# The scaled attention output is split by token, and a DMA transposes its halves

## The chip, the core and the metric

The kernel runs on one core of one Trainium2 chip. The metric is device time in microseconds (us) of one execution. Engines are named as in the profile: PE is TensorE, DVE is VectorE, ACT is ScalarE, POOL is GpSimd, and SP is the queue from which this kernel issues all its DMAs.

## The reference

Top-k attention over 4 batches, 8 heads, 576 tokens and a head width of 64, followed by two two-layer networks over the 2304 tokens (width 512, hidden width 2048):

```python
scores = scale * np.matmul(q, k.transpose(0, 1, 3, 2))
kth = np.partition(scores, -top_k, axis=-1)[..., -top_k:-top_k + 1]   # top_k = 32
scores = np.where(scores >= kth, scores, -1000000000.0)
attn = softmax(scores)                     # written out in the reference, with 1e-09 in the sum
x = (attn @ v) as (2304, 512)
x = np.maximum(x @ w_in1, 0.0) ** 2 @ w_out1
h = x @ w_in2
out = (h * np.clip(h + 3.0, 0.0, 6.0) / 6.0) @ w_out2
```

q, k and v are float32; the four weight matrices arrive as float64.

## The kernel before

**Precision.** Each matmul operand is scaled by a power of two and split into two fp16 halves, high and low; a product is the sum of three fp16 matmuls (high by high, high by low, low by high).

**Attention.** The tokens of a batch are cut into four blocks of 128 and one of 64. A block has 8 tiles (one head, 128 rows), a 64-token block 4 (two heads stacked): 144 tiles in all. A tile goes through PE (`qk`, L769), ACT (`evac`, L775), DVE (`topk`: four MAX8 and three MATCH_REPLACE8, L783 to L791, then `lowest`, L800), ACT (`below`, L805), POOL (`mask`, L808), ACT (`expo`, L813; `high`, L819), POOL (`low`, L823 and L824), a DMA transpose on SP (`wflip`, L828, into a buffer `wT`), and PE (`av`, L842).

**The operand of the first network.** `x_operand` turns a block's attention output into the operand `hl`, with features on the partitions. There are 20 blocks. Before the change: ACT copies the output head by head out of PSUM (L912), PE transposes it into a PSUM bank `misc` (`xflip`, L921), ACT squares it (L927), PE adds the squares over the features with four matmuls by a matrix of ones into a bank `h` (`xtotal`, L932), DVE takes the largest sum over the tokens (L936) and makes a power of two of it (L263 to L265), ACT scales the transposed values (L965) and makes the high half (L968), and POOL makes the low half (L971).

**The networks.** Two 64-token blocks share one unit, so there are 18 units of 128 tokens. For each unit `up` (L1091) makes four hidden blocks in one of the two PSUM banks `h`, ACT and DVE apply the function (L1098 to L1113), POOL makes the low half (L1116), and `acc` adds the second product (L1126 in the first network, L1134 in the second). Between the two networks `x2_operand` does for the unit what `x_operand` does for a block, without a transpose; its sum of squares is one matmul with one column (L1016).

**Weights.** At the start DVE turns the float64 words into float32 (L364 to L367) with help from ACT (L410) and POOL (L414), PE sums squares for a scale (L430), and PE, ACT and POOL split the matrices into halves.

**What sets the order.** `Plan` holds every step as a task with an engine, a cost and buffers to take, and runs through them with a priority from the table `PRIO` (an offset and a slope in the tile's or unit's number): whenever an engine is free, the ready task of lowest priority value whose buffers are free goes next. What comes out is a fixed order of instructions on each engine, SP included. On the chip each engine keeps that order, and an instruction that waits holds up everything behind it on its engine.

```python
    pool("wT", WTB, [P, 2 * S // P, P], F16)
    pool("x", XBUFS, [P, H, D], F32)
    for name, n in (("av", 1), ("misc", 1), ("h", 2)):
        pool(name, n, [P, 512], F32, ps)
```

Of the kernel before, what the change touches and what calls it, by code (L numbers as in the profile page):

```python
# [10 lines left out]
F16 = mybir.dt.float16  # L11
# [8 lines left out]
P = 128  # L20
# [12 lines left out]
class Plan:  # L33
# [101 lines left out]
def tile_topk_attention_moe_moe2(  # L135
# [36 lines left out]
    ones16 = const.tile([P, P], BF16, name="ones16")  # L172
    nc.gpsimd.memset(ones16, 1.0)
# [57 lines left out]
    pool("ghl", GBUFS, [P, 2, 512], F16)  # L231
    pool("m", 4, [P, TOPK], F32, st)
# [13 lines left out]
    def act(n):  # L246
        return 0.08 + 0.00086 * n
# [636 lines left out]
    def x_operand(i):  # L884
# [21 lines left out]
        def copy():  # L906
            box["x"] = x = take("x")
            a_ = T["av", i]
            for t in range(ntl):
                for hh in range(2 if tail else 1):  # L910
                    rows = slice(hh * TAIL, hh * TAIL + TAIL) if tail else slice(0, P)
                    nc.scalar.activation(x[0:n, 2 * t + hh if tail else t, :], a_[rows, t * D:(t + 1) * D], AF.Copy,  # L912
                                         scale=box["rv"][rows, t:t + 1])

        def flip():
            if o == 0:
                T["hl", u] = take("hl")
            box["pt"] = take("misc", "pt").rearrange("p (c n) -> p c n", c=KD)[:, :, 0:n]
            x = box["x"].rearrange("p h d -> p (h d)")
# [3 lines left out]
        def part(a):  # L923
            return T["hl", u][:, a, :, o:o + n]

        def square():
            nc.scalar.activation(part(1).bitcast(BF16), box["pt"], AF.Square)  # L927

        def total():
            box["pn"] = take("h", "pnx")[:, 0:n]  # L930
            for c in range(KD):
                nc.tensor.matmul(box["pn"], ones16, part(1).bitcast(BF16)[:, c, :], start=c == 0, stop=c == KD - 1)  # L932

        def scale():
            y = take("xy")
            nc.vector.tensor_reduce(y, box["pn"], axis=AX.X, op=ALU.max)  # L936
            T["sx", i], T["px", i] = take("scx"), take("px")
            scale_pair(y, T["px", i], EXP_P, T["sx", i])
# [6 lines left out]
        t3 = task("ACT", 1.6, ("xcopy", first[i]), copy, deps=[t2, *avs], alloc=["x"])  # L945
        free("rv", t1, t3)
        free("av", avs[0], t3)
        t4 = task("PE", 0.44 if not tail else 0.3, ("xflip", first[i]), flip, deps=[t3, hl_task.get(u)],
                  alloc=["misc"] + (["hl"] if o == 0 else []))
        hl_task.setdefault(u, t4)  # L950
        free("x", t3, t4)
        t5 = task("ACT", act(4 * n), ("xsquare", first[i]), square, deps=[t4])
        t6 = task("PE", mm(KD, n), ("xtotal", first[i]), total, deps=[t5], alloc=["h"])
        t7 = task("DVE", 0.65, ("xscale", first[i]), scale, deps=[t6], alloc=["xy", "scx", "px"])
        free("h", t6, t7)
        free("xy", t7, t7)
        scale_task[i] = t7
        if (SX if i else SX0) == "d":
            l_, = split(4 * n, lambda: box["pt"], [lambda: part(0)], [lambda: part(1)], lambda: T["sx", i], "d",
                        (("xhigh", first[i]), ("xlow", first[i])), [t7])  # L960
            free("misc", t4, l_)
        else:
            def evac():
                box["y"] = take("f", "y").rearrange("p (c n) -> p c n", c=KD)[:, :, 0:n]
                nc.scalar.activation(box["y"], box["pt"], AF.Copy, scale=T["sx", i])  # L965

            def high():
                nc.scalar.activation(part(0), box["y"], AF.Copy)  # L968

            def low():  # L970
                nc.gpsimd.tensor_tensor(part(1), box["y"], part(0), op=ALU.subtract)  # L971

            t8 = task("ACT", act(4 * n) + 0.09, ("xevac", first[i]), evac, deps=[t7], alloc=["f"])
            free("misc", t4, t8)
            t9 = task("ACT", act(4 * n), ("xhigh", first[i]), high, deps=[t8])
            l_ = task("POOL", gps(4 * n), ("xlow", first[i]), low, deps=[t9])
            free("f", t8, l_)
# [294 lines left out]
def first_of(order, b):  # L1272
# [16 lines left out]
SX = 'a'  # L1289
SX0 = 'a'  # L1290
# [3 lines left out]
WTB = 3  # L1294
# [9 lines left out]
    "load0": (79.38, 0.002),  # L1304
    "load1": (505.67, 1.218),
    "load2": (-131.52, 0.003),
    "load3": (-742.35, 0.015),
    "conv0": (-318.82, 2.010),
    "bits0": (15.78, 1.944),
    "add0": (40.24, 0.042),  # L1310
    "gram0": (150.09, 4.901),
    "conv1": (-402.12, 2.168),
    "bits1": (62.78, 1.548),
    "add1": (-314.29, 16.236),
    "gram1": (-177.84, 0.701),
    "conv2": (-322.11, 0.202),
    "bits2": (169.55, 0.060),
    "add2": (28.40, 0.397),
    "gram2": (37.78, 3.746),
    "conv3": (-319.50, 17.808),  # L1320
    "bits3": (-1197.31, 17.209),
    "add3": (-924.51, 132.166),
    "gram3": (-337.51, 0.363),
    "norm": (162.88, 3.211),
    "high0": (17.00, 4.877),
    "low0": (-407.54, 0.099),
    "scaled0": (1601.72, 0.274),
    "rest0": (124.60, 2.815),
    "high1": (39.66, 0.582),
    "low1": (363.86, 5.940),  # L1330
    "scaled1": (-638.88, 0.490),
    "rest1": (309.81, 6.499),
    "high2": (-353.82, 10.969),
    "low2": (525.93, 0.745),
    "scaled2": (1277.25, 0.112),
    "rest2": (497.91, 0.025),
    "high3": (328.67, 0.002),
    "low3": (323.86, 20.953),
    "scaled3": (12.56, 0.347),
    "rest3": (-296.43, 0.212),  # L1340
    "qsquare": (394.64, 3.096),
    "qtotal": (-522.30, 1.796),
    "qscale": (125.99, 6.115),
    "ksquare": (-651.27, 0.007),
    "ktotal": (-269.97, 0.040),
    "kscale": (60.65, 12.061),
    "vsquare": (-636.46, 0.206),
    "vtotal": (75.79, 0.095),
    "vscale": (1408.81, 257.879),
    "clear": (-435.69, 0.309),  # L1350
    "kload": (-205.24, 0.102),
    "vload": (360.66, 0.741),
    "qload": (-298.49, 5.036),
    "qhigh": (-487.53, 4.251),
    "qlow": (466.63, 0.760),
    "khigh": (-716.41, 2.774),
    "klow": (-745.17, 5.318),
    "vhigh": (-259.52, 0.835),
    "vlow": (371.44, 0.013),
    "kflip": (-237.83, 0.002),  # L1360
    "qscales": (357.31, 5.406),
    "qflip": (-3100.27, 1.015),
    "qk": (-92.22, 0.128),
    "evac": (-217.65, 0.005),
    "topk": (463.92, 4.188),
    "bias": (532.21, 0.398),
    "lowest": (-289.40, 0.274),
    "below": (6.46, 3.277),
    "mask": (-252.11, 1.195),
    "expo": (862.15, 0.942),  # L1370
    "whigh": (717.42, 0.312),
    "wlow": (749.09, 0.067),
    "wflip": (-709.67, 0.008),
    "av": (164.55, 0.248),
    "xinv": (692.76, 0.068),
    "xscales": (209.04, 12.568),
    "xcopy": (-199.03, 0.051),
    "xflip": (-261.41, 0.066),
    "xsquare": (-883.08, 0.591),
    "xtotal": (-1192.44, 0.731),  # L1380
    "xscale": (13.67, 0.378),
    "xevac": (-571.14, 1.046),
    "xhigh": (30.26, 0.684),
    "xlow": (-392.23, 0.138),
    "common": (166.36, 0.361),
    "ysquare": (37.42, 7.183),
    "ytotal": (-968.65, 0.540),
    "yscale": (-150.95, 4.882),
    "yhigh": (61.82, 2.649),
    "ylow": (-23.74, 0.008),  # L1390
    "whole": (37.32, 0.817),
    "up0": (568.05, 3.995),
    "up1": (500.02, 46.668),
    "relu0": (-966.40, 1.173),
    "relu1": (-180.07, 2.665),
# [39 lines left out]
```

## Time and profile before

| | |
|---|---|
| median of 3 runs | 1182.12 us (1181.19 to 1182.57) |
| the profiled execution | 1180.5 us |
| its span, first to last instruction | 1178.7 us |
| PE, DVE, ACT, POOL busy | 89%, 84%, 79%, 71% of the span |
| HBM read, written | 48.23 MB, 4.72 MB |

A busy share is the union of an engine's instructions. Matmuls overlap one another (each lasts some 0.2 us while a new one starts every 0.06 us), so the pace of PE is read from the distance between starts. The wait of an instruction is given behind it as the idle time of its engine and what ended it.

### The profile page before, as it was taken

How to read it: one execution, taken by the hardware profiler on the slowest of the kernel's cores; microseconds unless marked ns; L12 is line 12 of the kernel's file. 1: busy time of each engine (PE TensorE's matmuls, PEld its weight loads, DVE VectorE, ACT ScalarE, POOL GpSimd, SP SyncE). 2: the span in 40 equal slices, each digit the busy share in tenths (PEclk: the TensorE clock that was granted, in tenths of full speed). 3: DMA queues.
4: the chain of work that ended last, by engine and by line, in shares of the span. 5: the costliest groups of instructions: out<-in, count | busy, mean ns of one | idle time of the engine just before them, and what ended most of it. 6: DMA issues, size and time to landing. Idle time of an engine off the chain costs nothing.

```text
span 1178.7 us, 36919 instructions
## 1 busy us (share of the span) xinstructions
PE 1051.4 (89%) x14792; PEld 862.5 (73%) x14792; DVE 988.8 (84%) x2319; ACT 925.6 (79%) x1868; POOL 835.3 (71%) x1113
## 2 busy tenths in 40 slices
PE   2375688878999999999999999999989999999998
PEld 1232336776788788889787978888777978888885
DVE  4989899998995999999989999999978999998101
ACT  6589599899798878788888878888887787877432
POOL 5858868699775677777867787786766778777321
PEclk9997699988999999999999999999999999999999
DMA  9888754423554343445464443445463334333100
GB/s 235 234 249 244 225 156 119 104 48 65 90 97 102 79 75 55 75 74 98 78 118 84 71 74 56 72 62 92 86 110 55 66 65 80 62 60 61 12 11 19
DMA packets 276764, 112.50 MB, mean 95 GB/s; under 512 B 257520, under 2 KB 265712, under 8 KB 276592
## 3 DMA queue, kind: packets, MB, share of 16 engines
q1 hardware_dynamic: 276592, 110.14, 45.2%
q8 instruction: 116, 1.90, 0.7%
q14 instruction: 56, 0.46, 0.1%
HBM read 48.23 MB, written 4.72 MB: 45 GB/s over the span
## 4 chain that ended last, share of the span: by engine, by line
PE 53%; ACT 18%; DVE 9%; POOL 8%; issue 6%; DMA 5%; SPq 1%; ACTq 0%; DVEq 0%; POOLq 0%
PE hb L1091 21%; PE acc L1134 12%; PE acc L1126 11%; PE sp L769 4%; PE av L842 3%; POOL E L808 2%; ACT E L813 2%; DVE W L788 2%; ACT x L912 2%; POOL wc L823 2%; ACT S L775 2%; DVE m L791 1%; DVE cv L364 1%; DMA kT<-kn 1%; ACT w L541 1%
## 5 line engine op out<-in xcount | busy, mean ns | idle before, releaser
L1091 PE MATMUL hb<-hl,w 128*128 128x128 f16 x6912 | 456.2, 219 | 4.8 <-ACT stg L410 1.4
L1091 PEld LDWEIGHTS <-w 128*128 128x128 f16 x6912 | 411.4, 98 | 50.7 <-issue 6.4
L791 DVE MAX8 m<-W 128x8 f32<-128x576 f32 x432 | 326.0, 755 | 8.3
L1126 PE MATMUL acc<-ghl,w 128*128 128x128 f16 x3456 | 243.5, 221 | 5.3 <-ACT ghl L1113 2.6
L1134 PE MATMUL acc<-w,ghl 128*128 128x512 f16 x864 | 231.5, 379 | 11.7 <-DVE hl L279 7.5
L808 POOL TENSOR_TENSOR E<-S,E 128x576 f32<-128x576 f32 x144 | 204.3, 1419 | 48.5 <-ACT E L805 42.1
L1116 POOL TENSOR_TENSOR ghl<-r,ghl 128x512 f16<-128x512 f32 x144 | 169.4, 1177 | 93.5 <-ACT ghl L1113 85.3
L1126 PEld LDWEIGHTS <-w 128*128 128x128 f16 x3456 | 209.7, 99 | 17.6 <-issue 7.0
L788 DVE MATCH_REPLACE8 W<-m,W 128x576 f32<-128x576 f32 x288 | 213.8, 742 | 0.0
L823 POOL TENSOR_TENSOR wc<-E,wc 128x512 f16<-128x512 f32 x144 | 168.0, 1166 | 39.6 <-ACT wc L819 39.0
L775 ACT ACTIVATE S<-sp 128x576 f32<-128x576 f32 x144 | 93.5, 649 | 48.1 <-POOL E L808 40.0
L813 ACT ACTIVATE E<-E,scalars,scl 128x576 f32<-128x576 f32 x144 | 125.1, 869 | 4.4 <-POOL E L808 4.3
L805 ACT ACTIVATE E<-S,scalars 128x576 f32<-128x576 f32 x144 | 111.8, 776 | 19.0 <-DVE scalars L800 14.9
L783 DVE MAX8 m<-S 128x8 f32<-128x576 f32 x144 | 107.9, 750 | 18.9 <-ACT S L775 18.3
L769 PE MATMUL sp<-kT,qT 128*128 128x288 f16 (+1 forms) x640 | 100.1, 298 | 24.8 <-ACT S L775 20.0
L1134 PEld LDWEIGHTS <-ghl 128*128 128x128 f16 x864 | 74.9, 99 | 56.0 <-issue 16.0
L788 DVE MATCH_REPLACE8 W<-m,S 128x576 f32<-128x576 f32 x144 | 107.0, 743 | 0.0
L1106 DVE SCALAR_TENSOR_TENSOR r<-r,hb 128x512 f32<-128x512 f32 x72 | 49.0, 680 | 67.6 <-ACT r L1100 66.7
L1113 ACT ACTIVATE ghl<-r 128x512 f16<-128x512 f32 x144 | 90.5, 629 | 17.4 <-DVE r L1106 12.6
L819 ACT ACTIVATE wc<-E 128x576 f16<-128x576 f32 x144 | 98.5, 684 | 1.3
L795 POOL TENSOR_SCALAR scalars<-m,scl 128x1 f32<-128x1 f32 x144 | 38.5, 269 | 81.5 <-ACT E L813 32.2
L769 PEld LDWEIGHTS <-qT 128*128 128x128 f16 (+1 forms) x640 | 54.9, 103 | 51.8 <-issue 34.4
(130 smaller groups left out, 1493.5 us busy)
## 6 DMA issues: line engine op xcount, KB each, us to landing
w<-in_moe_w_in_dram SPq DMA_DIRECT2D x32, 512.0 KB, 4.9
w<-in_moe_w_out_dram SPq DMA_DIRECT2D x29, 512.0 KB, 4.4
out_dram<-o SPq DMA_DIRECT2D x16, 256.0 KB, 2.1
qf<-in_q_dram SPq DMA_DIRECT2D x31, 128.0 KB, 2.7
stg<-in_k_dram SPq DMA_DIRECT2D x12, 256.0 KB, 2.9
stg<-in_v_dram SPq DMA_DIRECT2D x12, 256.0 KB, 3.2
wT<-wc SPq DMA_TRANSPOSE x144, 3.2
stg<-in_moe_w_out_dram SPq DMA_DIRECT2D x6, 256.0 KB, 3.3
```

Source lines behind the costliest of these rows:

```text
L769: nc.tensor.matmul(dst, qT[:, 2 * ((2 * hp + hh) % 4) + a, 0:M], kflat[:, hh * SPAD + c * HALF:hh * SPAD + (c + 1) * HALF], start=a == 0, ...
L775: nc.scalar.activation(T["S", s].rearrange("p (c n) -> p c n", c=2), T["sp", s][:, :, 0:HALF], AF.Copy)
L788: nc.vector.match_replace(out=T["W", s], in_to_replace=m[:, 8 * c - 8:8 * c], in_values=T["S", s] if c == 1 else T["W", s], imm_value=-3.0e38)
L791: nc.vector.max(m[:, 4 * r:4 * r + 8], T["W", s])
L805: nc.scalar.activation(T["E", s], T["S", s], AF.Relu, bias=T["kb", s], scale=-FAR)
L808: nc.gpsimd.tensor_tensor(T["E", s], T["S", s], T["E", s], op=ALU.subtract)
L813: nc.scalar.activation(T["E", s], T["E", s], AF.Exp, bias=T["nb", s], scale=T["scl", ("q", i, half)][:, hp % 2:hp % 2 + 1], accum_out=T["s ...
L823: nc.gpsimd.tensor_tensor(wc[:, S + TAIL:], e[:, 0:S - TAIL], wc[:, 0:S - TAIL], op=ALU.subtract)
L1091: nc.tensor.matmul(box["h"][:, fi * n:(fi + 1) * n], wt[2 * m][:, kk * 4 + f // 4, a, f % 4 * P:(f % 4 + 1) * P], hl[:, c, kk, 0:n], start ...
L1116: nc.gpsimd.tensor_tensor(flat(box["g"][:, 1]), flat(box["r"]), flat(box["g"][:, 0]), op=ALU.subtract)
L1126: nc.tensor.matmul(flat_[:, c * w_:c * w_ + n], wt[1][:, f, a, c * P:(c + 1) * P], gl[d], start=(f, a, d) == (0, 0, 0) and c * w_ % 512 == ...
L1134: nc.tensor.matmul(o_, gl[d][:, ch * P:ch * P + rows], wt[3][:, f, a, :], start=f == 0 and (a, d) == (0, 0), stop=f == KF - 1 and (a, d) = ...
```

## The change

The operand keeps its tokens on the partitions until the end. ACT copies the output out of PSUM as before, squares all of it into a scratch tile and adds each token's squares on the way (`square`); PE adds the 128 tokens' sums with one matmul of one column (`total`), so that the norm is the sum of squares over the whole block instead of the largest token's; DVE makes the power of two (`scale`); ACT scales the copy in place (`scaled`) and makes the high half (`high`), POOL the low half (`low`), both into a new tile `xh`; and a DMA transpose on SP writes both halves, eight blocks of 128 by 128, into `hl` (`flip`). The transposes on PE and the DVE maximum are gone. `x` is held until `low` is done, the banks `misc` and `h` are taken for the one-column sum alone (`misc`) or not at all (`h`), and the buffers `wT` go from three to two. The path with `SX` is removed. All entries of `PRIO` are replaced.

```diff
+    pool("xh", XHBUFS, [P, 2, 512], F16)
...
+        def square():
+            box["xh"] = take("xh")
+            box["ss"] = take("ss")
+            nc.scalar.activation(box["xh"][0:n, 0].bitcast(BF16), rows(), AF.Square, accum_out=box["ss"][0:n])
+
+        def total():
+            box["pn"] = take("misc", "pnx")[:, 0:1]
+            nc.tensor.matmul(box["pn"], ones32[0:n, :], box["ss"][0:n], start=True, stop=True)
...
+        def scaled():
+            nc.scalar.activation(rows(), rows(), AF.Copy, scale=T["sx", i][0:n])
+
+        def high():
+            nc.scalar.activation(box["xh"][0:n, 0], rows(), AF.Copy)
+
+        def low():
+            nc.gpsimd.tensor_tensor(box["xh"][0:n, 1], rows(), box["xh"][0:n, 0], op=ALU.subtract)
+
         def flip():
...
-            for c in range(KD):
-                nc.tensor.transpose(box["pt"][:, c, :], x[0:n, c * P:(c + 1) * P], ident[0:n, 0:n])
...
+            nc.sync.dma_start_transpose(out=T["hl", u].rearrange("p a c n -> p (a c) n")[:, :, o:o + n],
+                                        in_=box["xh"][0:n].rearrange("p a n -> p (a n)"))
...
-        t6 = task("PE", mm(KD, n), ("xtotal", first[i]), total, deps=[t5], alloc=["h"])
+        t6 = task("PE", 0.2, ("xtotal", first[i]), total, deps=[t5], alloc=["misc"])
...
+        l_ = task("SP", 1.25, ("xflip", first[i]), flip, deps=[t10], lat=WLAT)
...
-WTB = 3
+WTB = 2
+XHBUFS = 1
...
-    "xflip": (-261.41, 0.066),
+    "xflip": (-58.53, 3.060),
```

**On PE**, where the last operand was transposed, before the change (`hb` and `acc` are the products of the second network of the units ahead; `w2`, `w3` its weights):

```order
L1091 LDWEIGHTS w2_88
L1091 MATMUL hb_20675<-hl_18739,w2_88 128x128
L921 MATMUL pt_20762<-ident_70,x_20718 128x128 x4
L1134 LDWEIGHTS ghl_20716
L1134 MATMUL acc_92<-w3_89,ghl_20716 128x512
```

And after the change, where the last operand's sum stands (L926 is the new `total`, L1080 and L1123 are the old L1091 and L1134):

```order
L1080 LDWEIGHTS w2_86
L1080 MATMUL hb_20537<-hl_18502,w2_86 128x128
L926 MATMUL pnx_20577<-scalars_83,ones32_75 128x1
L1123 LDWEIGHTS ghl_20471
L1123 MATMUL acc_90<-w3_87,ghl_20471 128x512
```

The four transposes, and the four matmuls by ones that followed some rows later, have become one matmul of one column.

**On SP**, near the end of the program, before the change (`wT` is a tile's transposed softmax weights, `o` the output of a unit):

```order
L828 DMA_TRANSPOSE wT_19735<-wc_19647 128x9x128
L828 DMA_TRANSPOSE wT_19849<-wc_19761 128x9x128
L828 DMA_TRANSPOSE wT_19994<-wc_19937 128x9x128
L1214 DMA out_0_dram<-o_20051 128x512
L828 DMA_TRANSPOSE wT_20102<-wc_20068 128x9x128
```

And after the change, with the operand of the block before the last (L942 is the new `flip`, L827 the old L828):

```order
L827 DMA_TRANSPOSE wT_19667<-wc_19617 128x9x128
L942 DMA_TRANSPOSE hl_19588<-xh_19623 128x8x128
L827 DMA_TRANSPOSE wT_19791<-wc_19727 128x9x128
L1203 DMA out_0_dram<-o_19854 128x512
L827 DMA_TRANSPOSE wT_19897<-wc_19831 128x9x128
```

The operand's transpose stands between two tiles' transposes, which wait behind it.

**On DVE**, around the scale of the first operand, before the change (`m` and `W` are of `topk`, `cv` of the weights' conversion, `w3` holds words of the last matrix):

```order
L791 MAX m_1430<-W_1531 128x8
L800 TENSOR_SCALAR scalars_85<-m_1430 128x1
L364 TENSOR_SCALAR cv_1620<-w3_89 128x512
L788 MATCH_REPLACE W_1623<-m_1508,S_1444 128x576
L367 SCALAR_TENSOR_TENSOR w3_89<-w3_89,cv_1620 128x512
L936 TENSOR_REDUCE scalars_85<-pnx_1626 128x1
L263 TENSOR_SCALAR scalars_85<-scalars_85 128x1
```

And after the change (L262 reads the one-column sum; L782 to L790 are `topk`):

```order
L790 MAX m_884<-W_968 128x8
L782 MAX m_1172<-S_992 128x8
L799 TENSOR_SCALAR scalars_83<-m_884 128x1
L787 MATCH_REPLACE W_1180<-m_963,S_946 128x576
L262 TENSOR_SCALAR scalars_83<-pnx_1183 128x1
L363 TENSOR_SCALAR cv_1199<-w3_87 128x512
L366 SCALAR_TENSOR_TENSOR w2_86<-w3_87,cv_1199 128x512
```

The scale stands earlier in the sequence of tiles, in front of conversions of the third matrix instead of the fourth, and the TENSOR_REDUCE ahead of it is gone.

## Rows read from the trace of the kernel before

**Rows 1.** The page, parts 1 and 2: busy shares, then tenths in 40 slices.

```profile
PE 1051.4 (89%) x14792; PEld 862.5 (73%) x14792; DVE 988.8 (84%) x2319; ACT 925.6 (79%) x1868; POOL 835.3 (71%) x1113
...
PE   2375688878999999999999999999989999999998
...
DVE  4989899998995999999989999999978999998101
```

**Rows 2.** Windows: length, then busy us (instructions) by engine, granted clock, DMA.

```profile
core 0: us, PE busy (x) PEld busy (x) DVE busy (x) ACT busy (x) POOL busy (x), PEclk, DMA share, GB/s
0.00:300.00 300.00, 200.56 (x1986) 137.71 (x1988) 262.15 (x599) 245.40 (x486) 232.29 (x288) 0.92 0.63 166
300.00:1090.00 790.00, 767.67 (x11708) 658.16 (x11708) 715.74 (x1693) 649.77 (x1327) 581.27 (x802) 1.00 0.44 78
1090.00:1178.70 88.70, 83.13 (x1105) 66.67 (x1102) 10.94 (x28) 30.46 (x56) 21.74 (x25) 0.99 0.07 14
```

**Rows 3.** Timeline of PE, 505 to 522: start, length, instruction, count.

```profile
508.75 0.83 PE L1126 MATMUL acc<-ghl,w 128*128 128x128 f16 x12
509.42 0.83 PE L1091 MATMUL hb<-hl,w 128*128 128x128 f16 x12
510.09 0.61 PE L921 MATMUL pt<-ident,x 128*128 128x128 f32 x4
510.54 0.65 PE L769 MATMUL sp<-kT,qT 128*128 128x288 f16 x4
...
511.70 0.39 PE L932 MATMUL pnx<-hl,ones 128*128 128x128 bf16 x4
511.92 0.83 PE L1126 MATMUL acc<-ghl,w 128*128 128x128 f16 x12
...
514.82 0.28 PE L1016 MATMUL pnx<-scalars,ones 128*128 128x1 f32 x2
514.96 1.46 PE L1134 MATMUL acc<-w,ghl 128*128 128x512 f16 x6
```

**Rows 4.** Windows for L921 alone: length, then busy us (instructions).

```profile
0.00:300.00 300.00, 2.57 (x12) 1.47 (x12) 0.92 0.63 166
300.00:1178.70 878.70, 10.16 (x68) 7.12 (x68) 1.00 0.40 71
```

**Rows 5.** Timeline of all engines, 1100.5 to 1110: the last operand's steps.

```profile
1101.01 1.73 ACT L912 ACTIVATE x<-av,rv 128x64 f32<-128x64 f32 x8
...
1103.81 0.67 ACT L927 ACTIVATE hl<-pt 128x512 bf16<-128x512 f32 x1
...
1105.90 0.29 DVE L936 TENSOR_REDUCE scalars<-pnx 128x1 f32<-128x128 f32 x1 [1.19 <-PE pnx L932]
1106.22 0.15 DVE L263 TENSOR_SCALAR scalars<-scalars 128x1 int32<-128x1 int32 x1
...
1106.66 0.69 ACT L965 ACTIVATE y<-pt,scalars 128x512 f32<-128x512 f32 x1 [1.28 <-DVE scalars L265]
1107.38 0.63 ACT L968 ACTIVATE hl<-y 128x512 f16<-128x512 f32 x1
1108.08 1.16 POOL L971 TENSOR_TENSOR hl<-y,hl 128x512 f16<-128x512 f32 x1 [1.47 <-ACT hl L968]
```

**Rows 6.** The same, 507.5 to 518: first and last step of an operand in mid-run.

```profile
507.92 1.73 ACT L912 ACTIVATE x<-av,rv 128x64 f32<-128x64 f32 x8
...
516.80 1.16 POOL L971 TENSOR_TENSOR hl<-y,hl 128x512 f16<-128x512 f32 x1
```

**Rows 7.** The page, part 6: DMA transposes, count, median us from issue to landing.

```profile
wT<-wc SPq DMA_TRANSPOSE x144, 3.2
...
qT<-kn SPq DMA_TRANSPOSE x40, 3.1
```

**Rows 8.** Timeline of SP, 940 to 975: one tile's transpose.

```profile
942.46 1.29 SPq L828 DMA_TRANSPOSE wT<-wc  x1
```

**Rows 9.** Timeline of PE, 940 to 975: products with `wT`, tile after tile.

```profile
943.00 0.57 PE L842 MATMUL av<-vv,wT 128*128 128x64 f16 x14
...
950.28 0.57 PE L842 MATMUL av<-vv,wT 128*128 128x64 f16 x14
...
958.09 0.57 PE L842 MATMUL av<-vv,wT 128*128 128x64 f16 x14
```

**Rows 10.** Groups by line: busy us, mean ns of one, idle before and its releasers.

```profile
L791 DVE MAX8 m<-W 128x8 f32<-128x576 f32 x432 | 326.0, 755 | 8.3
L1010 ACT ACTIVATION_READ_ACCUMULATOR hl<-acc 128x1 f32 x16 | 3.3, 205 | 0.0
```

More of the change, by code (lines that the diff above doesn't have):

```diff
@@ L907, in copy @@
             box["x"] = x = take("x")
+            if o == 0:
+                T["hl", u] = take("hl")
             a_ = T["av", i]
@@ new lines, in x_operand @@
+        t5 = task("ACT", act(H * D), ("xsquare", first[i]), square, deps=[t3], alloc=["xh", "ss"])
+        t6 = task("PE", 0.2, ("xtotal", first[i]), total, deps=[t5], alloc=["misc"])
+        free("ss", t5, t6)
+        t7 = task("DVE", 0.34, ("xscale", first[i]), scale, deps=[t6], alloc=["scx", "px"])
+        free("misc", t6, t7)
+        scale_task[i] = t7
+        t8 = task("ACT", act(H * D) + 0.09, ("xevac", first[i]), scaled, deps=[t7])
+        t9 = task("ACT", act(H * D), ("xhigh", first[i]), high, deps=[t8])
@@ L978, in x_operand @@
+        t10 = task("POOL", gps(H * D), ("xlow", first[i]), low, deps=[t9])
+        free("x", t3, t10)
+        l_ = task("SP", 1.25, ("xflip", first[i]), flip, deps=[t10], lat=WLAT)
+        free("xh", t5, l_)
         opd_task.setdefault((0, u), []).append(l_)
@@ L1320 @@
[L1320 to L1335, printed above, removed]
@@ new lines @@
+    "bits1": (5400.69, 0.172),
+    "add1": (-1385.37, 5.018),
+    "gram1": (183.03, 103.357),
+    "conv2": (17.45, 1.125),
+    "bits2": (493.63, 6.855),
+    "add2": (-194.01, 0.089),
+    "gram2": (-26.79, 0.004),
+    "conv3": (616.59, 11.533),
+    "bits3": (159.55, 0.665),
+    "add3": (-2.72, 1.332),
+    "gram3": (-262.91, 4.417),
+    "norm": (-1365.91, 0.363),
+    "high0": (288.05, 0.305),
+    "low0": (644.96, 1.940),
+    "scaled0": (101.97, 0.013),
+    "rest0": (902.25, 1.044),
@@ new lines @@
+    "qscales": (411.78, 0.077),
+    "qflip": (-726.93, 0.309),
+    "qk": (147.76, 2.327),
+    "evac": (837.53, 12.809),
+    "topk": (5592.52, 0.472),
+    "bias": (600.17, 0.206),
+    "lowest": (196.71, 0.209),
+    "below": (128.10, 2.341),
+    "mask": (29.16, 0.029),
+    "expo": (832.44, 0.963),
+    "whigh": (26.42, 4.490),
+    "wlow": (1849.78, 0.018),
+    "wflip": (165.58, 0.019),
+    "av": (70.95, 0.369),
+    "xinv": (482.49, 3.583),
+    "xscales": (-76.34, 0.518),
+    "xcopy": (-683.24, 0.090),
@@ new lines @@
+    "xflip": (-58.53, 3.060),
+    "xsquare": (-74.37, 0.039),
+    "xtotal": (-62.25, 0.841),
+    "xscale": (177.05, 0.181),
+    "xevac": (81.03, 0.139),
+    "xhigh": (-51.91, 3.563),
+    "xlow": (1309.70, 0.398),
+    "common": (-311.74, 2.790),
+    "ysquare": (5377.34, 2.395),
+    "ytotal": (-667.52, 0.159),
+    "yscale": (-137.53, 3.765),
+    "yhigh": (5.49, 0.661),
+    "ylow": (-99.64, 0.946),
+    "whole": (266.47, 0.009),
+    "up0": (501.58, 0.258),
+    "up1": (611.57, 1.002),
@@ L1407 @@
+    "relu0": (4480.76, 0.137),
+    "relu1": (-113.70, 0.001),
+    "gsquare": (4441.59, 2.346),
+    "gate": (1104.75, 0.727),
+    "ghigh0": (841.11, 0.914),
+    "ghigh1": (-518.27, 2.118),
+    "glow0": (1024.96, 0.372),
+    "glow1": (-121.02, 2.062),
+    "acc0": (-3.24, 0.053),
+    "acc1": (613.66, 1.000),
+    "oscale": (80.93, 0.314),
+    "oevac": (97.64, 0.808),
+    "store": (4437.04, 6.159),
 }
```

184 lines of the change are left out of this document (50 added, 134 removed).

## The prediction

> **What bounds the kernel now.** I read the page first, then the windows, then the timelines. On the page PE is busy 89% of the span and DVE 84%, and the tenths show when: DVE is at 9 from the second slice of 29.5 us until the attention ends, PE only from about the tenth slice on, and then it stays there to the end [rows 1]. The windows make two stages of it. Up to 300 us PE is busy for 200.56 us and DVE for 262.15; weights are converted, and there is too little ready work for PE. From 300 to 1090 PE is busy 767.67 of 790 us, 97%, and DVE 715.74, 91%; after that DVE has almost nothing to do and PE is busy 83.13 of 88.70 us [rows 2]. Busy does not yet mean full pace, since matmuls overlap. The timeline shows the pace: a group of 12 matmuls of 128 columns starts 0.67 us after the group before it (508.75 and 509.42) with other work directly behind [rows 3]. So after 300 us work taken off PE shortens the run almost one for one, as long as DVE, with some 74 us to spare in that stage, keeps up. Work taken off ACT, DVE or POOL there is worth little by itself.
>
> **PE's work.** For each of the 20 blocks the change removes four transposes and four matmuls by ones. Start to start with the next row the transposes take 510.54 - 510.09 = 0.45 us and the sums 511.92 - 511.70 = 0.22 us. What is added is one product with one column, in the form that the second network's norm has already: 514.96 - 514.82 = 0.14 us [rows 3]; I take 0.17, since its weights are float32 and one row tells little. Net 0.50 us a block. Of the 80 transposes 68, those of 17 blocks, lie behind 300 us [rows 4]: 17 x 0.50 = 8.5 us, and 8 us with the four half-sized blocks among them. Bounds: 0 if PE only waits instead, 10 us if all 20 count.
>
> **DVE.** Twenty maxima of 0.29 us [rows 5] go, 5.8 us in all, and with them the step that read a bank `h`, which the `up` groups need. Behind 300 us DVE has slack, so this is worth nothing there; before 300 us DVE is the engine that sets when operands are ready.
>
> **The start.** The priorities are all new, so I counted in the order of DVE how many instructions of `topk` stand ahead of each operand's scale. First operand: 100 before, 66 now; second 139 and 128; third 204 and 194; fourth 253 and 252; last 1008 and 1008. At 0.755 us each [rows 10] the first is some 26 us earlier in DVE's work and the second and third some 8 us, but the fourth only 0.8. PE becomes the bound at about the fourth. So what lasts is 0.8 us and the four maxima gone by then, 1.2 us: 2 us. Bounds: 8 us gained, if the early operands let PE build a lead that it keeps; 8 us lost, if the new order of loads, conversions and tiles waits more than the old one, which no row can tell.
>
> **The operand's way.** This gets longer. In the last block it runs from 1101.01 to 1109.24, 8.2 us; in a block in mid-run from 507.92 to 517.96, 10.0 us [rows 5, 6]. Its pure work in the last block is 1.73 + 0.45 + 0.67 + 0.22 + 0.29 + 0.45 + 0.69 + 0.63 + 1.16 = 6.3 us [rows 3, 5] (0.45 the second time for three small DVE steps of 0.15), so 1.9 to 3.7 us are waits for a turn. The new way is 1.73 + 0.67 + 0.20 (reading the accumulator [rows 10]) + 0.17 + 0.45 + 0.69 + 0.63 + 1.16 = 5.7 us, and then the DMA. That moves the same eight blocks of 128 by 128 as the transposes of q, which land 3.1 us after issue, and one less than those of the softmax weights, 3.2 us [rows 7]. With waits for a turn as before and up to 1.3 us behind another transpose on SP [rows 8] the operand is there 10.7 to 13.8 us after the last `av`.
>
> What covers this is what PE has to do meanwhile, and the new order has more of it. Between the last tile's `av` and the first `up` of the last unit stood 11 groups (some 0.66 us each, with the transposes and sums 8.2 us); now 21 groups stand there, 14.3 us. For the other units behind 300 us the same count gives 9.5 to 16.4 us before, mostly 10, and 12.5 to 21.3 now, mostly 15. So I cost the DMA's latency at nothing: 14.3 to 15 us of `up` and `acc` work hide 10.7 to 13.8. With that cover gone it costs 18 us (one for each unit) for each us that it is late.
>
> The Trainium skill (VectorE: DVE Perf Modes, sections "The three transpose paths" and "Rules for kernel authors") advises the opposite of this change: a 128 by 128 transpose belongs on TensorE when PSUM will do, with 390 ns there against 1309 ns through the DMA crossbar. The trace agrees that TensorE's takes less, but its eight-block DMA transposes in 3.1 us [rows 7] show that blocks do not take 1.3 us one after another. By the page's figure as a price per block the DMA would be an estimated 10.5 us.
>
> **Two `wT` instead of three.** A tile's transpose was issued at 942.46 [rows 8]; its product ran at 950.28, until 950.85. The products come at 943.00, 950.28 and 958.09, one in 7.5 us [rows 9]. A buffer is held 8.4 us, and two of them allow 15: no cost in mid-run. At the start tiles come less evenly, which the 8 us above take in.
>
> **SP.** Twenty more transposes of 1.3 us are 26 us of a queue that mostly waits. Each waits for POOL's `low`, and the softmax transposes of the next tiles wait behind it, then `av` on PE. In the tile above the weights landed at about 942.46 + 3.2 = 945.7, 4.6 us before their turn on PE [rows 7 to 9]; a hold of that size is hidden.
>
> **ACT and POOL.** Four more us on ACT (20 x 0.20) in 79% busy, the same POOL work; hidden.
>
> **The sum.** Against the profiled execution: 1180.5 - 8 - 2 = 1170.5 us. The median of the runs shown is 1.6 us above it, so I forecast 1172 us, with 1163 to 1178 as this case's own range: the two bounds of the start, without the part that PE's gain could lose. No change means within 0.2%, 1179.8 to 1184.5 us, about what a measurement of this kernel can tell.
>
> **The rivals.**
>
> *The operand is late (slower).* The place is SP's queue between `low` and the first `up` of every unit. For: the margin is 0.5 to 4 us only, and in the old order the cover in the last block, 8.2 us of groups, was no longer than the operand's way of 8.2 us, so such orders are cut close. Against: the counts above. It decides at 10 / 18 = 0.6 us late in the mean over the units, where the gain is used up; 1.5 us late gives 1172 + 27 = 1199. Chance 0.12.
>
> *Blocks go one after another (slower).* The destination of this transpose, a unit's `hl`, is not that of any row. The rows bound the price of a block from above by the whole DMA, 3.1 us [rows 7]. If its eight blocks went in turn at a quarter of that, 6.2 us in all, the way takes 13.8 to 15.6 us and comes out late by up to 1 us; at the full price, 24.8 us, it is 17 us late in each of 18 units, 1172 + 306 = 1478. Against: nine blocks land in 3.2 us and eight in 3.1. Chance 0.02. The page's rule on transposes above is this mechanism; by its figure it would be an estimated 3 to 6 us late in each unit, some 1226 to 1280 us.
>
> *The new order waits more (slower).* The start is 300 us long with 99 us of PE idle [rows 2]; a tenth more of it, 10 us, and the 8 us lost at the start give 1172 + 18 = 1190. The point of decision is 10 us of new waits. Nothing in the counts points there: operands are never later in DVE's order. Chance 0.13.
>
> *Nothing is left.* PE's 8 us turn into waits for DVE. The 74 us of DVE's slack speak against, the fixed order on both engines, in which small waits follow from each other, for it: 1180 to 1184. Chance 0.12.
>
> *The lead holds (faster yet).* The first unit starts its matmuls some 26 us earlier, PE fills part of its 99 idle us, and DVE's 74 us of slack behind 300 are waits for PE that shrink. A sixth of the idle time gives 1172 - 16 = 1156. Chance 0.18.
>
> **The numbers.** The forecast has 0.43. Faster: 0.43 + 0.18 and the better half of the waits' case that stays under 1179.8, about 0.02, makes 0.63; same 0.12 and slower 0.25 (0.12, 0.02, and 0.11 of the third). The range, 1153 to 1190 us, reaches a little below the lead's 1156 and to the 1190 of the new order's waits; it leaves out the late operand, the blocks in turn, and the far ends of those two cases, some 0.2 together.
>
> **What will show it.** If right: no L921 and no four-matmul sums on PE, its busy time behind 300 us close to the length of the stage, a transpose into `hl` landing in about 3.1 us, waits of `hb` for that DMA in sum under 5 us, waits of SP for `av` near nothing in mid-run, and the attention's last top-k on DVE a few us earlier. Wrong would be: PE idle before `hb` with the DMA into `hl` as the releaser, unit after unit; `av` waiting for `wT`; or the fourth operand ready later than before.

## The result and the profile after

The changed kernel takes 1171.42 us, the median of four runs (1169.59 to 1173.15), against 1182.34 us for the kernel before, also four runs. The ratio is 0.9909 with an interval from 0.9895 to 0.9924, so the change saves 10.9 us (9.0 to 12.4). The forecast was 1172 us in a range from 1153 to 1190.

The profiled execution of the changed kernel took 1173.15 us with a span of 1171.4 us; it is the longest of the four. Its page, part 1, answers to [rows 1]:

```profile
PE 1045.9 (89%) x14672; PEld 857.2 (73%) x14672; DVE 983.0 (84%) x2299; ACT 924.2 (79%) x1888; POOL 835.6 (71%) x1112
```

PE is busy 5.5 us less than before (1051.4). What is left of a span is PE's idle time: 1178.7 - 1051.4 = 127.3 us before, 1171.4 - 1045.9 = 125.5 us now. So the profiled spans differ by 7.3 us, of which 5.5 is busy time gone and 1.8 is idle time gone. Windows over the stages of [rows 2], in the same columns, show that the idle time also moved:

```profile
0.00:300.00 300.00, 205.76 (x2032) 141.44 (x2033) 268.04 (x608) 249.02 (x497) 237.87 (x294) 0.93 0.66 171
300.00:1090.00 790.00, 765.46 (x11677) 656.41 (x11674) 705.28 (x1668) 646.90 (x1341) 581.07 (x803) 1.00 0.46 82
1090.00:1171.40 81.40, 74.65 (x975) 59.37 (x971) 9.68 (x24) 28.28 (x51) 16.70 (x16) 0.99 0.05 15
...
620.00:628.00 8.00, 6.30 (x43) 4.20 (x41) 6.30 (x15) 3.70 (x7) 2.93 (x5) 0.57 0.49 103
```

Up to 300 us PE idles 94.2 us where it idled 99.4: 5.2 less. From 300 to 1090 it idles 24.5 us where it idled 22.3, and in the last stage 6.75 where it idled 5.57: 3.4 more in these two. The last row is a stretch in which the granted clock falls to 0.57 of full speed in the mean; the section at the end comes back to it, since it adds to the busy time of this one execution. The run with DVE's maximum put back (among the experiments) has the same matmuls in the same order and no such fall behind 300 us. Its span is 1170.4 us and PE is busy 1042.1, so against before 9.3 us of busy time are gone (a part of it at the start, where the granted clock is 0.94 there and 0.92 before) and the idle time is 0.9 us longer. What the two executions agree on is that PE's busy time fell and that its idle time is about what it was: less at the start, more later.

The operand's way can be followed on the last block, as [rows 5] did. The timeline of all engines, start and length first:

```profile
1089.69 0.57 PE L841 MATMUL av<-vv,wT 128*128 128x64 f16 x14
1090.35 1.75 ACT L913 ACTIVATE x<-av,rv 128x64 f32<-128x64 f32 x8 [2.46 <-PE av L841]
1092.12 0.63 ACT L922 ACTIVATE xh<-x 128x512 bf16<-128x512 f32 x1
1092.66 0.19 ACT L922 ACTIVATION_READ_ACCUMULATOR xh<-x 128x1 f32 x1
1092.90 0.38 PE L926 MATMUL pnx<-scalars,ones 128*128 128x1 f32 x2
...
1095.22 1.16 POOL L939 TENSOR_TENSOR xh<-x,xh 128x512 f16<-128x512 f32 x1 [6.11 <-ACT xh L936]
1096.40 1.23 SPq L942 DMA_TRANSPOSE hl<-xh  x1
...
1105.87 1.34 PE L1080 MATMUL hb<-hl,w 128*128 128x128 f16 x21
```

The copy begins 10.7 us earlier than in [rows 5]. The tile `hl` seen by itself, its products on PE and the transpose that writes it:

```profile
L1080 PE MATMUL hb<-hl,w x6912: 216/219/314, 160.9 to 1161.3; 128*128 128x128 f16 x198
L942 SPq DMA_TRANSPOSE hl<-xh x20: 1194/1233/2206, 135.3 to 1096.4; - x20
...
DMA to landing us min/median/max: 2.7/3.1/4.9
```

Before, the first of these lines read:

```profile
L1091 PE MATMUL hb<-hl,w x6912: 216/220/231, 189.8 to 1168.4; 128*128 128x128 f16 x198
```

With the median landing the last operand is there at 1096.40 + 3.1 = 1099.5, some 9 us after the last `av`, and its first `up` stands at 1105.87. PE has other work for the 6.4 us between. The view of waits on PE and of the SP queue (us in total, times, longest):

```profile
PE sp L768 <- ACT S L774: 18.4, 13, 6.6
PE acc L1123 <- DVE hl L278: 7.9, 10, 1.1
```

```profile
SPq L827 <- PE av L841: 51.1, 34, 6.3
```

No wait of `hb` for the DMA into `hl` appears among PE's. On SP there is a wait that before came once and for 1.9 us, of the softmax transposes for an `av` that must first free one of the two buffers `wT`.

To see when the gain comes, the first copy of each operand (L913, before L912) is a good mark. Before, the timeline of ACT has three operands from the first half of the run at

```profile
219.18 1.74 ACT L912 ACTIVATE x<-av,rv 128x64 f32<-128x64 f32 x8
...
334.91 1.73 ACT L912 ACTIVATE x<-av,rv 128x64 f32<-128x64 f32 x8
...
404.45 2.60 ACT L912 ACTIVATE x<-av,rv 64x64 f32<-64x64 f32 x8 [0.33 <-POOL wc L824]
```

and after the change at

```profile
210.44 1.72 ACT L913 ACTIVATE x<-av,rv 128x64 f32<-128x64 f32 x8
...
327.43 1.69 ACT L913 ACTIVATE x<-av,rv 128x64 f32<-128x64 f32 x8
...
393.63 2.55 ACT L913 ACTIVATE x<-av,rv 64x64 f32<-64x64 f32 x8
...
607.67 1.72 ACT L913 ACTIVATE x<-av,rv 128x64 f32<-128x64 f32 x8
...
888.94 2.56 ACT L913 ACTIVATE x<-av,rv 64x64 f32<-64x64 f32 x8 [0.64 <-PE av L841]
```

The first three are 8.7, 7.5 and 10.8 us earlier than those of before, and the last one of all, in the timeline above, 10.7 us. (607.67 and 888.94 serve the experiments.) The distance is there by the second operand, and over the 880 us from it to the last it grows by about 2 us only. Part of the distance is order and not time: more `up` and `acc` work now stands behind an operand than before, which is why the last copy is 10.7 us earlier and the end only 7.3.

### The profile page after: what moved, and what is told of

Same layout as the page of the kernel before. It is cut to its first block, busy times and chain, and to the rows that moved or that the text cites. A ratio compares the mean times of both kernels' runs of the same rounds, so it can differ in the third digit from the quotient of the medians.

```text
span 1171.4 us, 36695 instructions
## 1 busy us (share of the span) xinstructions
PE 1045.9 (89%) x14672; PEld 857.2 (73%) x14672; DVE 983.0 (84%) x2299; ACT 924.2 (79%) x1888; POOL 835.6 (71%) x1112
## 4 chain that ended last, share of the span: by engine, by line
PE 52%; ACT 19%; DVE 9%; POOL 8%; issue 6%; DMA 5%; SPq 1%; POOLq 0%; ACTq 0%; DVEq 0%
PE hb L1080 20%; PE acc L1123 12%; PE acc L1115 10%; PE av L841 3%; PE sp L768 3%; DVE W L787 2%; ACT E L812 2%; POOL E L807 2%; DVE m L790 2%; ACT wc L818 2%; ACT E L804 1%; DMA kT<-kn 1%; ACT x L913 1%; POOL ghl L1105 1%; ACT w L546 1%
## 5 line engine op out<-in xcount | busy, mean ns | idle before, releaser
L1080 PE MATMUL hb<-hl,w 128*128 128x128 f16 x6912 | 457.3, 220 | 7.3 <-ACT r L1087 5.0
L1080 PEld LDWEIGHTS <-w 128*128 128x128 f16 x6912 | 416.0, 99 | 50.2 <-issue 10.3
L790 DVE MAX8 m<-W 128x8 f32<-128x576 f32 x432 | 325.8, 754 | 8.1
L1105 POOL TENSOR_TENSOR ghl<-r,ghl 128x512 f16<-128x512 f32 x144 | 167.6, 1166 | 108.4 <-ACT ghl L1102 104.3
L1123 PE MATMUL acc<-w,ghl 128*128 128x512 f16 x864 | 231.4, 381 | 15.0 <-DVE hl L278 7.9
L1115 PE MATMUL acc<-ghl,w 128*128 128x128 f16 x3456 | 239.6, 219 | 2.6 <-POOL ghl L1105 1.9
L1123 PEld LDWEIGHTS <-ghl 128*128 128x128 f16 x864 | 75.3, 99 | 62.3 <-issue 20.0
L768 PE MATMUL sp<-kT,qT 128*128 128x288 f16 (+1 forms) x640 | 100.1, 298 | 22.3 <-ACT S L774 18.4
L782 DVE MAX8 m<-S 128x8 f32<-128x576 f32 x144 | 108.1, 751 | 7.3 <-ACT S L774 6.5
L841 PEld LDWEIGHTS <-wT 128*128 128x128 f16 (+1 forms) x2240 | 83.0, 103 | 13.6 <-issue 6.2
L841 PE MATMUL av<-vv,wT 128*128 128x64 f16 (+1 forms) x2240 | 91.8, 196 | 0.0
```

Of the source, the lines that this page charges most:

```text
L768: nc.tensor.matmul(dst, qT[:, 2 * ((2 * hp + hh) % 4) + a, 0:M], kflat[:, hh * SPAD + c * HALF:hh * SPAD + (c + 1) * HALF], start=a == 0, ...
L790: nc.vector.max(m[:, 4 * r:4 * r + 8], T["W", s])
L841: nc.tensor.matmul(out_[cols, t * D:(t + 1) * D], wT[0:kr, a, cols], vv[0:kr, vb, hh, c, :], start=n_ == 0, stop=n_ == len(prods) - 1)
L1080: nc.tensor.matmul(box["h"][:, fi * n:(fi + 1) * n], wt[2 * m][:, kk * 4 + f // 4, a, f % 4 * P:(f % 4 + 1) * P], hl[:, c, kk, 0:n], start ...
L1105: nc.gpsimd.tensor_tensor(flat(box["g"][:, 1]), flat(box["r"]), flat(box["g"][:, 0]), op=ALU.subtract)
L1115: nc.tensor.matmul(flat_[:, c * w_:c * w_ + n], wt[1][:, f, a, c * P:(c + 1) * P], gl[d], start=(f, a, d) == (0, 0, 0) and c * w_ % 512 == ...
```

## The experiments

Each kernel was timed against the kernel before. "Over after" is the difference of two ratios to the kernel before, times 1182 us; each ratio is known to some 2 us, a difference of two to some 3.

**PE's work put back.** Four transposes and four matmuls by ones go back on PE ahead of each operand's sum, on constant data; nothing else moves.

```diff
+            for _ in range(1):
+                for c in range(KD):
+                    nc.tensor.transpose(bank[:, c * P:c * P + n], ident[0:n, :], ident[0:n, 0:n])
+                for c in range(KD):
+                    nc.tensor.matmul(bank[:, 0:n], ones, ones[:, 0:n], start=c == 0, stop=c == KD - 1)
             nc.tensor.matmul(box["pn"], ones32[0:n, :], box["ss"][0:n], start=True, stop=True)
```

> The changed kernel, its order untouched, with four transposes and four matmuls by ones of no use put back on PE ahead of each operand's sum (their result is overwritten). If the gain is PE's removed work: 0.45 + 0.22 = 0.67 us for each of the 17 operands behind 300 us, the four half ones counted less, +10 to +11 us, 1181 to 1183. Rival, the gain is the new order with its earlier start and PE's work is absorbed by waits: at most +3 us, 1174 or less.

It took 1179.54 us, ratio 0.9964 (0.9949 to 0.9979): 6.5 us over after, between the two expectations. With `range(2)` in place of `range(1)`:

> The same with eight transposes and eight matmuls by ones. If PE's time counts one for one: +20 to +23 us, 1191 to 1195, twice the step of the single one. Rival: the step of the second is smaller than that of the first, or both stay under 6 us, 1177.

That took 1193.06 us, ratio 1.0077 (1.0057 to 1.0097): 20 us over after, and 13.4 over the single dose. 20 blocks at 0.45 + 0.22 us [rows 3] are 13.4 us, so the second dose costs its full work. The first does not. Windows from 300 us to the end say why. They have the columns of [rows 2] and show the run with the maximum put back (the same order without a dose), the single dose and the double one; the granted clock is 1.00 in all three:

```profile
300.00:1170.37 870.37, 838.30 (x12651) 714.28 (x12649) 717.81 (x1711) 675.76 (x1392) 598.16 (x820) 1.00 0.42 76
300.00:1177.52 877.52, 850.40 (x12834) 727.24 (x12831) 718.25 (x1699) 678.96 (x1396) 601.44 (x823) 1.00 0.42 75
300.00:1190.25 890.25, 861.36 (x12952) 737.06 (x12949) 719.40 (x1696) 678.78 (x1395) 600.54 (x821) 1.00 0.42 74
```

The idle time of PE there is 32.1, 27.1 and 28.9 us. The first dose adds 12.1 us to PE's busy time and takes 5.0 us from its idle time; the second adds 11.0 busy and 1.8 idle. In this order PE waits some us whether or not it has those transposes to do, and the first dose fills a part of these waits. So the removed work is real time, but 6.5 us of it in this order, not 10. The dose is the 0.67 us that the change takes from PE in each block, without the one-column product that it adds; the change's net gain on PE is therefore below 6.5 us. The cost comes all along the run: the copies of operands fall behind those of after by 0.8 us at the second (211.22), 3.0 at the tenth (610.63) and 6.0 at the last (1096.31).

**DVE's maximum put back.**

```diff
+            nc.vector.tensor_reduce(T["px", i], ident[:, 0:n], axis=AX.X, op=ALU.max)
             scale_pair(box["pn"], T["px", i], EXP_P, T["sx", i])
```

> The changed kernel, its order untouched, with a maximum of 128 by 128 on DVE put back ahead of each operand's scale (of a constant, its result is overwritten). If DVE has slack behind 300 us: 0 to +1.5 us, 1171 to 1173 (the first three operands count at most 0.9 us). Rival, DVE paces the whole attention: 20 x 0.28 = +5.6 us, 1177.

1172.95 us, ratio 0.9916 (0.9892 to 0.9940): 0.8 us over after, inside what can be told from nothing. The maximum was worth nothing that shows.

**The order alone.** The kernel before, all its steps kept, with the new table `PRIO` (one line of some hundred):

```diff
-    "xflip": (-261.41, 0.066),
+    "xflip": (-58.53, 3.060),
```

> The kernel before with nothing changed but its table of priorities, which is the changed kernel's; the operand is still transposed on PE, with three buffers wT. If the gain comes from the removed PE work, this one does not have it: 1180 or more. Rival, the gain is the priorities' earlier start: 1171 to 1175.

1213.72 us, ratio 1.0247 (1.0221 to 1.0272): 29 us slower than before. Its timeline of ACT, the operands that stand above at 334.91 and 404.45:

```profile
330.96 1.75 ACT L912 ACTIVATE x<-av,rv 128x64 f32<-128x64 f32 x8
...
426.72 2.59 ACT L912 ACTIVATE x<-av,rv 64x64 f32<-64x64 f32 x8
```

The first is 4 us early (7.5 in the changed kernel), the second 22 us late: between them lies the first change of batch. The new numbers alone bring an earlier start and lose it, and more, behind that. The old steps do not fit them: the number for `xflip`, made for a DMA on SP, here places the transposes on PE. So this run does not price the order by itself, and the new steps in the old order were not run: the order and the steps are not priced apart.

**A longer transpose.** Each operand's DMA transpose is issued twice, then three times, into the same place.

```diff
+            for _ in range(2):
+                nc.sync.dma_start_transpose(out=T["hl", u].rearrange("p a c n -> p (a c) n")[:, :, o:o + n],
+                                            in_=box["xh"][0:n].rearrange("p a n -> p (a n)"))
```

> The changed kernel with each operand's DMA transpose issued twice, the same data to the same place. In the changed kernel's trace the operand lands 2.4 to 8.3 us ahead of the unit's first matmul in 17 of 18 units (and 22.6 in the first). The second transpose lands 1.3 us later (issue time alone) or 3.1 us later (if it waits for the first). If the cover holds: shortfalls of 0 to 1.7 us in sum, 1171 to 1174. Rival, no margin: 18 units x 1.3 to 3.1 us, +23 to +56 us, 1194 to 1227.

1190.49 us, ratio 1.0057 (1.0035 to 1.0079): 17.5 us over after, which is neither expectation. Its view of `hl`, and its waits on SP:

```profile
L943 SPq DMA_TRANSPOSE hl<-xh x40: 1194/1232/2153, 135.9 to 1118.2; - x40
...
  DMA hl<-xh: 0.9, 1
...
DMA to landing us min/median/max: 2.7/3.1/4.7
```

```profile
SPq L943 <- DMA hl<-xh: 36.9, 20, 3.5
```

The second copy waits on SP for the first to land, so `hl` is complete about 3 us later, and SP stands 36.9 us in sum for it. PE waits for it 0.9 us, once: the latency was covered, as forecast, and the 17.5 us have another cause. The copies of operands show where they arise:

```profile
330.79 1.70 ACT L913 ACTIVATE x<-av,rv 128x64 f32<-128x64 f32 x8
...
400.87 2.56 ACT L913 ACTIVATE x<-av,rv 64x64 f32<-64x64 f32 x8
...
620.04 1.73 ACT L913 ACTIVATE x<-av,rv 128x64 f32<-128x64 f32 x8
...
906.45 2.57 ACT L913 ACTIVATE x<-av,rv 64x64 f32<-64x64 f32 x8 [0.64 <-PE av L841]
...
1109.04 1.75 ACT L913 ACTIVATE x<-av,rv 128x64 f32<-128x64 f32 x8 [2.46 <-PE av L841]
```

Against after they are 3.4, 7.2, 12.4, 17.5 and 18.7 us late. These are steps at the start and at the changes of batch, and between them little. There SP has the loads of the next batch's k and v in its queue. Two loads of k at the second change of batch, first after, then with the doubling:

```profile
571.90 0.62 SPq L636 DMA_DIRECT2D stg<-in_k_dram  x1
587.89 0.70 SPq L636 DMA_DIRECT2D stg<-in_k_dram  x1
```

```profile
579.34 0.51 SPq L636 DMA_DIRECT2D stg<-in_k_dram  x1
600.10 0.74 SPq L636 DMA_DIRECT2D stg<-in_k_dram  x1
```

The one is 7.4 us late, as the copies ahead of it are; the other 12.2, about as the copy that follows.

> The same three times. If each waits for the one before, the operand is 6.2 us later, more than the margin of 13 units, shortfalls of 32 us in sum if nothing catches up: 1190 to 1204. If they follow back to back, 2.6 us later: 0 to 1 us by the margins, 1171 to 1174. Rival, no margin: 18 x 2.6 to 6.2 us, +47 us or more, 1218 and up.

1260.19 us, ratio 1.0654 (1.0630 to 1.0677): 88 us over after, in the range of the rival. Here the cover is used up. PE's waits:

```profile
PE hb L1081 <- DMA hl<-xh: 32.3, 14, 4.8
...
PE av L841 <- DMA wT<-wc: 13.4, 8, 3.9
```

The margins counted in the changed kernel's trace gave 32 us of waits for 6.2 us more of latency, and 32.3 is what came: the waits are those of the expectation, the total is not. Another 13.4 us are waits of `av` for softmax transposes, which stand behind on SP. A further part is the clock: PE is busy 1073.6 us where it is busy 1045.9 after, with the same 14672 matmuls, and the mean granted clock of the span is 0.950 against 0.979. These 27.7 us and 57.3 us more of idle time make up the 85.0 us between the two spans (1256.4 and 1171.4); 11.6 us of the idle time were not separated.

**Two DMAs of four blocks for one of eight.**

```diff
+            for a in range(2):
+                nc.sync.dma_start_transpose(out=T["hl", u][:, a, :, o:o + n], in_=box["xh"][0:n, a])
```

> The changed kernel with each operand's transpose as two DMAs of four blocks, one for each half. If a transpose is mostly a fixed time: each lands in 2.7 to 3.1 us, the second 1.2 us of issue later, within the margins, 1171 to 1174. Rival, blocks go one after another at an even share of the 3.1 us or more: each lands in 1.6 us or less.

1175.08 us, ratio 0.9930 (0.9911 to 0.9949): 2.5 us over after, which is within the noise, with one more issue per operand on SP. Each lands as the view of `hl` says:

```profile
DMA to landing us min/median/max: 2.3/2.5/4.1
```

The median is a little below the 2.7 to 3.1 expected and far above the rival's 1.6.

**Where the doubling costs.** It is done in the 9 blocks far from any load of k and v, and in the other 11.

```diff
-            for _ in range(2):
+            for _ in range(2 if first[i] in (40, 48, 72, 80, 88, 112, 120, 128, 136) else 1):
```

> The doubled transpose in 9 of the 20 blocks only, those that stand far from the loads of k and v (first tiles 40, 48, 72, 80, 88, 112, 120, 128, 136). Doubling all 20 cost some 18 us, though `hb` waited for the DMA 0.9 us in sum. If that cost comes from SP being held while the k and v of the next batch are due: 0 to +2 us over the changed kernel, 1171 to 1174. Rival, every doubled transpose costs the same, by lateness or otherwise: 18 x 9/20 = +8 us, 1179.

> The other 11 blocks doubled: those of the start (first tiles 0, 8, 16) and those around the changes of batch (24, 32, 36, 56, 64, 96, 104, 108). If SP's hold ahead of the k and v loads is the cause: +15 to +18 us, 1186 to 1190. Rival, the same cost for every block: 18 x 11/20 = +10 us, 1181.

Far: 1175.08 us, ratio 0.9926 (0.9911 to 0.9942), 2.0 us over after, not to be told from it. Near: 1186.53 us, ratio 1.0033 (1.0017 to 1.0049), 14.7 us over after. Together 16.7 of the 17.5. The near case's copies have steps in the same places, 6.6, 9.3 and 13.7 us behind after:

```profile
400.26 2.55 ACT L913 ACTIVATE x<-av,rv 64x64 f32<-64x64 f32 x8
...
617.00 1.73 ACT L913 ACTIVATE x<-av,rv 128x64 f32<-128x64 f32 x8
...
902.59 2.56 ACT L913 ACTIVATE x<-av,rv 64x64 f32<-64x64 f32 x8 [0.64 <-PE av L841]
```

**The loads moved off SP.** The k and v loads of batches 1 to 3 are issued from ACT, with single and with doubled transposes.

```diff
-                nc.sync.dma_start(f[:, :, 0:NFULL, :], src_[b, 2 * hp:2 * hp + 2, 0:NFULL * P, :]
+                (nc.scalar if b else nc.sync).dma_start(f[:, :, 0:NFULL, :], src_[b, 2 * hp:2 * hp + 2, 0:NFULL * P, :]
```

> The changed kernel with the loads of k and v of batches 1 to 3 issued from ACT at the place that they have in the plan, instead of SP. If SP's order holds up the change of batch in the changed kernel too: some us faster, 1164 to 1170. Rival, SP is not in the way as long as transposes are single, or ACT's own waits hold the loads up as much: 1171 to 1178.

> All transposes doubled, and the loads of k and v of batches 1 to 3 issued from ACT. If the doubled transposes cost what they do by holding those loads up on SP: most of the 14 us behind the start come back, at most +8 us over the same kernel with single transposes. Rival, the cost is elsewhere (the transposes of k, q and the softmax weights, which stay on SP): +12 us or more.

Single: 1183.49 us, ratio 1.0006 (0.9987 to 1.0024), 11.5 us over after and above both expectations. That the loads now wait for their turn in ACT's order is the likely reason; it is not shown. Doubled: 1191.47 us, ratio 1.0070 (1.0053 to 1.0088). The doubling costs 7.6 us here and 17.5 with the loads on SP, so some 10 us of its price, known to about 4, went with those loads. The copies of operands agree: between the two runs here they are 8.2 us apart at the sixth (401.26 and 409.48) and 9.9 at the last (1101.21 and 1111.13), so the steps at the second and third change of batch are nearly gone. A rival remains in part: the single run is itself late by then, which can hide some of a doubling. What makes up the 7.6 us was not separated; it is there by the sixth operand, at the first change of batch.

**Two buffers `wT` in the kernel before**, its order untouched.

```diff
-            T["wT", s] = take("wT")
+            shape, dtype, where = size["wT"]
+            T["wT", s] = where.tile(shape, dtype, tag=f"wT{s % 2}", name="wT", bufs=1)
```

> The kernel before, its order untouched, with tiles taking turns in two buffers wT instead of three. In its trace the third was needed by 2 of 144 tiles, tile 2 and tile 10, which would have had to wait 18 and 14.5 us on SP. If mid-run needs two only: 0 to +8 us, all of it ahead of 300 us, 1182 to 1190. Rival, two buffers hold tiles up throughout: av or SP waits in most tiles and +10 us or more, 1192.

1197.42 us, ratio 1.0118 (1.0100 to 1.0137): 14 us slower than before, a total in the range of the rival; but the place is the start, as expected. Windows, and the longest wait on SP:

```profile
0.00:120.00 120.00, 54.37 (x253) 27.89 (x254) 83.88 (x196) 77.01 (x148) 71.09 (x92) 0.91 0.74 210
...
300.00:1090.00 790.00, 766.25 (x11556) 653.05 (x11554) 715.21 (x1700) 650.78 (x1336) 583.52 (x808) 1.00 0.44 78
```

```profile
SPq L829 <- PE av L843: 78.1, 28, 22.0
```

In the first 120 us DVE is busy 83.88 us, where the same window of the kernel before has 98.61: one softmax transpose waits 22.0 us for an `av`, and the loads of the weights stand behind it on SP. From 300 to 1090 PE is as busy as in [rows 2] (766.25 against 767.67). The first operand is 15.0 us late, the last 17.9. So with an order made for three buffers the third is needed at the start and nearly nowhere else.

## Why the prediction was right, step by step

**The total** was right to 0.6 us, and its direction for the reason given: PE is the bound, and PE has less to do. The closeness is partly luck: two of its terms were off in size, in opposite directions, and a third effect was left out. PE's removed work accounts for at most 6.5 of the 10.9 us. That the rest is the new order's, with its earlier start, is argued from what is left over and not shown by a run of its own.

**PE's work, 8 us: the work is right, the price was too high.** In the run with the maximum put back, which has no stretch of low clock behind 300 us, PE is busy 1042.1 us, 9.3 us less than before; 20 x 0.50 = 10 was counted. But the experiment that puts the work back gives 6.5 us, known to some 3, for all 20 blocks, and that for 0.67 us a block where the term has 0.50, since 5.0 us of it vanish in idle time that PE has in any case. "Almost one for one" holds for the second dose and not for the first. The product that was added is also dearer than the 0.17 us counted: from its start to the next it takes 0.24 us in the median of the 17 behind 300 us.

**The start, 2 us: too low.** The step that failed is "PE becomes the bound at about the fourth. So what lasts is 0.8 us and the four maxima". I let only the fourth operand's place in DVE's order count. PE's idle time up to 300 us fell by 5.2 us in the profiled execution (by 3.2 in the run with the maximum put back), its first `up` stands at 160.9 us instead of 189.8, and PE did fill idle time with work that otherwise comes later. The upper bound, "8 us gained, if the early operands let PE build a lead that it keeps", and the rival of the lead describe the mechanism; its size, 3.2 to 5.2 us, lies between the term's 2 us and that bound, far from the rival's 16 us. The order alone brings operands earlier: the kernel before with the new table has them so too, up to the first change of batch.

**Left out: waits that come back later.** PE idles 3.4 us more behind 300 us (4.1 in the run with the maximum put back). That is the rival "nothing is left", PE's gain turning into waits, at about half of its size; whether they are waits for DVE, as it says, was not separated. With 5.5 us less busy time and 5.2 us less idle time at the start this gives the 7.3 us between the two profiled spans.

**DVE's maxima at nothing**: right, 0.8 us within 2. **The last top-k on DVE a few us earlier**: its last search (L790) begins at 1073.74, before at 1084.53, 10.8 us earlier.

**The operand's way and its cover**: right. The DMA lands in 3.1 us, and no `hb` waits for it. The last operand took about 9 us instead of the 10.7 to 13.8 allowed, and the cover of 14.3 us is 15.6 in the trace (1090.26, the end of the last `av`, to 1105.87). Doubling showed the margin to be about 3 us or more nearly everywhere; tripling showed where it ends. The rival of the late operand was right about the place, SP's queue, but the first thing to suffer there is not the operand. It is the loads behind it. Its price, 18 us for each us late, was not tested by itself: the tripling has 32.3 us of waits of `hb` in 14 places, among other losses.

**Blocks in turn**: refuted by the landing times. The Trainium skill (VectorE: DVE Perf Modes, section "The three transpose paths") gives 1309 ns for a 128 by 128 transpose of bf16 through the DMA. The runs here, of fp16, have 2.5 us for four blocks and 3.1 us for eight, so that figure is no price per block. The Trainium skill (VectorE: DVE Perf Modes, section "Rules for kernel authors") would have a 128 by 128 transpose on TensorE where PSUM will do. This is not borne out here, where PE is the bound and the DMA's latency is covered: with the DMA in place, putting PE's part back costs 6.5 us.

**Two `wT`**: half right. Mid-run it costs little even in the old order, where the last operand is 2.9 us later than the first one's 15.0. "Waits of SP for `av` near nothing in mid-run" is wrong: of 34 waits and 51.1 us, 31 and 44.7 us lie between 300 and 1090. The old order with two buffers, which waits 39.7 us for `av` on SP in that stage, shows such waits to be nearly free. At the start two buffers cost 15 us in the old order; the new one starts earlier with the same two.

**Two sums of the prediction do not come out.** In the rival of the blocks in turn, 6.2 us for the DMA give a way of 13.8 to 16.9 us with the 1.3 us behind another transpose, not 15.6. And the start's bounds, 8 us gained or lost where 2 us gained are in the sum, give 1166 to 1182 us and not 1163 to 1178. Neither moves the forecast.

**What stays open**: how much of the gain belongs to the new steps and how much to the new table, since the table alone is slower and the steps alone were not run; and the 7.6 us of doubling that the loads do not explain.

## What to carry to other kernels

Ask of an added DMA not only whether its result is late, but what stands behind it in its queue: here 3 us more latency cost PE 0.9 us of direct waits, while the whole doubling cost 17.5 us, 14.7 of them in the blocks near the start and near input loads that stand behind it. Price work taken off a bound engine as its time minus the waits that it was filling; a second dose put on tells the full price, the first only the net one. Where two executions differ in the granted clock, compare busy times only in stretches where it is the same. When a change replaces an order as well as steps, run the order alone before crediting either.

## What the runs showed that was not expected

**A DMA transpose is mostly fixed time.** From issue to landing it takes 2.5 us for four blocks of 128 by 128 in the median, 3.1 for eight and, in [rows 7], 3.2 for nine. From four to eight that is 0.15 us a block; by that an estimated 1.9 us do not depend on the number of blocks.

**A short fall of the clock.** In the changed kernel's profiled run the granted clock is 0.57 from 620 to 628 us, a mean between the full level (2.4 GHz) and half of it (1.2 GHz), and 1.00 before and after. PE waited several times around its beginning. Its timeline:

```profile
619.21 1.02 PE L1123 MATMUL acc<-w,ghl 128*128 128x512 f16 x3
621.00 1.44 PE L1123 MATMUL acc<-w,ghl 128*128 128x512 f16 x3 [0.78 <-ACT hl L274]
623.36 1.44 PE L1123 MATMUL acc<-w,ghl 128*128 128x512 f16 x3 [0.92 <-DVE scalars L799]
624.60 4.33 PE L1080 MATMUL hb<-hl,w 128*128 128x128 f16 x48
628.77 0.57 PE L841 MATMUL av<-vv,wT 128*128 128x64 f16 x14
```

The 48 matmuls take 4.17 us from start to start, where [rows 3] have 12 in 0.67, so 48 in 2.7: 1.5 us lost in this group alone. The waits do not explain the fall by themselves: in the run with the maximum put back PE waits the same 0.78 and 0.92 us ahead of these two `acc` groups, the granted clock stays at 1.00, and the 48 matmuls take 2.68 us. What decided between the two executions stays open.
